# Attention in pairs of units with a written order on every engine, half of expert 0 by seven products, and Sinkhorn steps between matmuls

## The chip, the cores and the metric

The kernel runs on one core of a Trainium2 chip. Its engines are TensorE (PE, with its weight loads shown apart as PEld), VectorE (DVE), ScalarE (ACT), GpSimd (POOL) and SyncE (SP, which only issues transfers here). The metric is device microseconds of one execution. Rows of a profile or trace call a line of the kernel L and its number.

## The reference

Attention, then a mixture of experts whose weights are normalised over rows and columns (Sinkhorn), then a second mixture with two experts for each token. All in float32.

```python
# attention: batch 2, heads 8, sequence 576, head dim 64
scores = scale * np.matmul(q, k.transpose(0, 1, 3, 2))
mask_local = (rel >= 0) & (rel < stride)                      # heads 0-3, stride 32
mask_strided = (rel >= 0) & (pos[None, :] % stride == pos[:, None] % stride)   # heads 4-7
...
attn = attn / (np.sum(attn, axis=-1, keepdims=True) + 1e-09)
x = attention output as (1152, 512)
# first mixture: 8 experts, w1 512x1024, w2 1024x512
P = np.exp(logits)
for _ in range(8):
    P /= P.sum(1, keepdims=True) + 1e-09
    P /= P.sum(0, keepdims=True) + 1e-09
    P *= N / E
for e in range(E):
    h = np.maximum(x @ w1[e], 0.0)
    ye = h @ w2[e]
    out += P[:, e:e + 1] * ye
# second mixture: the same sizes, noisy gate, the two best experts of each token
```

## The kernel before, in words

Every float32 product is made of three products of rounded operands: `split` (L101 to L106) writes the rounded part of a tensor on ACT (`hi`: xh, u1h, gh, ...) and the rest on DVE (`lo`: xl, u1l, gl, ...), and `mm3` (L164) multiplies hi by hi, lo by hi and hi by lo.

**Attention.** The (batch, two heads) blocks are cut into 24 units, 12 of local heads (3 blocks of 96 keys, 288 columns of scores) and 12 of strided heads (4 or 3 blocks of 54 keys, 216 or 162 columns). A unit (`unit`, L210 to L247) runs in this order: scores on PE (`sc`), the negated maximum and its scale on DVE (L231, L232), exponentials with row sums on ACT (L235), two small operations for the reciprocal on DVE (L236, L237), the multiplication by it on POOL (L238), transposes on PE (`tr`, L241), their copy to SBUF on DVE (`at`, L213), the product with the values on PE (`ot`, L247), and the split of the result into xh and xl. Ahead of the scores of the first units stand products of a constant that nobody reads (`hum`, L210): 10 and then 2 for each of the units 1 to 12, 32 in all.

**First mixture.** Expert 0 needs no Sinkhorn weight yet (its weight is multiplied in later, when expert 1 starts). Each expert's 1024 hidden columns are worked in 4 quarters of 256. A quarter of expert 0 is direct: `pair1` makes h (72 products of 384 columns, or as many in other widths), `pair2` makes y (54 products of 512 columns) and adds it to `acc` on DVE. Its tokens 0 to 511 are worked while the second batch's attention runs, the others after it. The quarters of experts 1 to 6 go by a scheme with seven products in place of eight (`Unit`, L665: 84 products of 288 columns for a quarter, and the same 54 of `pair2`). It needs four sums of quarters of x (`sums`: 16 additions on DVE, L622 and L624, then splits into sh and sl) and differences of weights made on POOL (`conv_wino`, L154). Expert 7 and the second mixture follow in another form, which the change leaves alone.

**Gate and Sinkhorn.** `gate_logits` (L320, L324) and `sinkhorn` (L329 to L353) run at a raised priority among expert 0's late tokens. One of the 8 rounds is nine small DVE operations around one product on PE, the column sum `cs` (L348). The small constants (`cs<-in_cst`, another `cs`) are loaded in two transfers; the second one, and `wg_sb`, are issued on ACT's queue at L298 after the ninth unit's split.

**Order.** A scheduler that simulates the program decides the order of each engine's instructions; priorities (`high_priority`) and `issue_after` marks steer it. Each engine runs its own instructions in that order.

## Time and profile before

| what | value |
|---|---|
| three runs | 1116.22, 1117.54, 1119.85 us; median 1117.54 us |
| the profiled execution: its span | 1120.2 us (no other time of it is listed) |
| PE busy | 1102.6 us (98%) |
| DVE, ACT, POOL busy | 665.0, 394.3, 173.8 us |
| attention, gate, Sinkhorn and expert 0 | about the first 175 us |

The span runs from the first to the last instruction of the profiled execution. Busy shares are means over all stages; PE's 98% includes stretches in which it was granted half its clock, and matmuls whose modelled ends overlap. The three runs spread over 0.3%.

### The profile page before, as it was taken

What the parts mean: (1) busy time and instruction counts of PE and PEld (TensorE: products, weight loads), DVE (VectorE), ACT (ScalarE), POOL (GpSimd) and SP (SyncE); (2) the same over time, 40 slices, a digit from 0 to 9 for tenths busy, and PEclk for the clock granted to TensorE, in tenths of its full rate; (3) what the DMA queues carried; (4) which work ended last, traced back from release to release, by engine and by line L of the source; (5) the groups of instructions that cost most, each with busy time, mean ns of one, the idle gap of its engine ahead of it and who ended that gap; (6) DMA issues with size and microseconds to landing.
All of it is one profiled execution on the core that took longest, in us unless ns stands there. A gap on an engine that the chain in (4) does not pass through costs nothing.

```text
span 1120.2 us, 17350 instructions
## 1 busy us (share of the span) xinstructions
PE 1102.6 (98%) x6878; PEld 957.3 (85%) x6878; DVE 665.0 (59%) x1374; ACT 394.3 (35%) x884; POOL 173.8 (16%) x204
## 2 busy tenths in 40 slices
PE   9899999999999999999999999999999999999996
PEld 5677989899998999899999989998888888888885
DVE  5785697666666666666666767553366364544440
ACT  5542144333332333323333323231123263544441
POOL 2110022111112111121111110000041431322211
PEclk9899999999999999999999999999999999999999
DMA  9512135112111121111111111022113682555541
GB/s 278 151 57 75 38 103 159 38 38 75 39 38 38 39 76 38 38 39 38 45 69 38 38 39 56 20 75 75 47 49 88 174 303 41 197 196 194 170 102 23
DMA packets 31216, 96.27 MB, mean 86 GB/s; under 512 B 6522, under 2 KB 15226, under 8 KB 22556
## 3 DMA queue, kind: packets, MB, share of 16 engines
q1 hardware_dynamic: 16028, 78.13, 20.6%
q0 software_dynamic: 5200, 10.17, 4.3%
q10 hardware_dynamic: 9904, 6.83, 2.0%
q8 instruction: 55, 0.90, 0.3%
q14 instruction: 29, 0.24, 0.1%
HBM read 83.60 MB, written 11.60 MB: 85 GB/s over the span
## 4 chain that ended last, share of the span: by engine, by line
PE 87%; DVE 4%; issue 3%; DMA 3%; POOL 2%; ACT 1%; POOLq 0%; ACTq 0%; SPq 0%
PE y L164 40%; PE h L164 16%; PE a L665 14%; PE b L665 7%; PE d L665 3%; PE y L838 2%; PE xgt L750 1%; DMA table<-en,si 1%; PE sc L225 1%; POOL table L498 1%; PE sc L210 1%; PE tr L241 1%; DMA wg_sb<-in_wg 1%; PE ot L247 1%; DMA xg<-x2d,tt 1%
## 5 line engine op out<-in xcount | busy, mean ns | idle before, releaser
L591 DVE SCALAR_TENSOR_TENSOR acc<-y,P,acc 128x512 f32<-128x512 f32 x207 | 152.6, 748 | 141.7 <-PE y L164 141.7
L164 PE MATMUL y<-u2h,gh 128*128 128x512 f32 x504 | 198.3, 394 | 0.3 <-DVE acc L591 0.3
L164 PE MATMUL y<-u2l,gh 128*128 128x512 f32 x504 | 197.1, 391 | 0.0
L164 PE MATMUL y<-u2h,gl 128*128 128x512 f32 x504 | 189.9, 392 | 0.7 <-DVE gl L102 0.6
L154 POOL TENSOR_TENSOR ut<-raw 128x256 f32<-128x256 f32 x48 | 35.6, 762 | 513.2 <-DVE u1l L106 442.0
L164 PEld LDWEIGHTS y<-u2h,gl 128*128 128x128 f32 x504 | 94.3, 188 | 20.9 <-DVE gl L102 2.0
L164 PE MATMUL h<-xl,wh 128*128 128x384 f32 (+8 forms) x352 | 110.2, 313 | 0.0
L164 PE MATMUL h<-xh,wh 128*128 128x384 f32 (+8 forms) x352 | 109.6, 315 | 0.3 <-DVE hl L102 0.3
L164 PE MATMUL h<-xh,wl 128*128 128x384 f32 (+8 forms) x352 | 109.8, 312 | 0.0
L164 PEld LDWEIGHTS y<-u2h,gh 128*128 128x128 f32 x504 | 94.7, 188 | 15.4 <-issue 0.7
L164 PEld LDWEIGHTS y<-u2l,gh 128*128 128x128 f32 x504 | 94.6, 188 | 13.9
L101 ACT ACTIVATE hh<-h 128x256 fp32r<-128x256 f32 (+2 forms) x88 | 35.5, 415 | 97.8 <-PE h L164 97.7
L164 PEld LDWEIGHTS h<-xh,wh 128*128 128x128 f32 x352 | 66.2, 189 | 2.1 <-DVE hl L102 0.6
L164 PEld LDWEIGHTS h<-xl,wh 128*128 128x128 f32 x352 | 66.4, 189 | 1.1 <-issue 0.6
L104 ACT ACTIVATE u2h<-raw 128x1024 fp32r<-128x1024 f32 x31 | 32.8, 1059 | 96.2 <-PE y L164 96.2
L164 PEld LDWEIGHTS h<-xh,wl 128*128 128x128 f32 x352 | 66.3, 188 | 0.0
L102 DVE SCALAR_TENSOR_TENSOR hl<-h,hh 128x256 fp32r<-128x256 f32 (+2 forms) x88 | 40.4, 464 | 38.9 <-ACT hh L101 38.9
L106 DVE TENSOR_TENSOR wl<-raw,wh 128x1024 fp32r<-128x1024 f32 x42 | 49.6, 1221 | 18.7 <-ACT wh L104 18.7
L665 PE MATMUL b<-sh,u1h 128*128 128x288 f32 x192 | 56.9, 296 | 0.0
L665 PE MATMUL a<-sh,u1l 128*128 128x288 f32 x192 | 56.9, 296 | 0.0
L665 PE MATMUL b<-sl,u1h 128*128 128x288 f32 x192 | 56.8, 296 | 0.0
L665 PE MATMUL a<-sl,u1h 128*128 128x288 f32 x192 | 56.7, 295 | 0.0
(248 smaller groups left out, 2502.5 us busy)
## 6 DMA issues: line engine op xcount, KB each, us to landing
raw<-in_u SPq DMA_DIRECT2D x31, 1024.0 KB, 5.0
raw<-in_v SPq DMA_DIRECT2D x20, 1024.0 KB, 10.3
acc<-in_v SPq DMA_DIRECT2D x12, 1024.0 KB, 7.5
raw<-in_w SPq DMA_DIRECT2D x4, 1024.0 KB, 5.3
out<-zero ACTq DMA_DIRECT2D x1, 3072.0 KB, 18.7
x2d<-acc ACTq DMA_DIRECT2D x9, 256.0 KB, 2.0
vs<-in_vL SPq DMA_DIRECT2D x4, 432.0 KB, 11.4
ks<-in_kS SPq DMA_DIRECT2D x4, 297.0 KB, 7.7
```

The lines of the kernel that those rows point to most:

```text
L101: seen[0] = nc.scalar.activation(hi, src, AF.Relu)
L102: nc.vector.scalar_tensor_tensor(lo, src, 0.0, hi.bitcast(F32), op0=ALU.max, op1=ALU.subtract)
L104: seen[0] = nc.scalar.activation(hi, src, AF.Copy)
L106: nc.vector.tensor_tensor(lo, src, hi.bitcast(F32), op=ALU.subtract)
L154: nc.gpsimd.tensor_tensor(t[:, o], x, y, op=ALU.subtract)
L164: nc.tensor.matmul(o, a, b, start=start, stop=stop)
L210: nc.tensor.matmul(o, onesb, onesb[:, None, :].to_broadcast([128, 4, 128]), start=True, stop=True)
L225: nc.tensor.matmul(sc[h * 64:h * 64 + w, i * nk:(i + 1) * nk], qs[r, j * w:(j + 1) * w], ks[r, j * step:j * step + nk], start=False, stop= ...
L241: nc.tensor.transpose(tr[:nk, i * nq:(i + 1) * nq], s[:, i], ident[:nq, :nq])
L591: nc.vector.scalar_tensor_tensor(acc[:, t], p, P[:, t, scale:scale + 1], acc[:, t], op0=ALU.mult, op1=ALU.add)
L665: nc.tensor.matmul(p, l[:, b, c], m, start=first and i == 0, stop=i == 5, skip_group_check=not first)
L838: nc.tensor.matmul(p[j * w:j * w + k, :d], hr[:, f, :k], raws[f // 4][:, f % 4, j * d:(j + 1) * d], start=f == 0, stop=f == 7)
```

## The change

- Attention runs in 12 pairs of units with methods (`Pair`, `Piece`) whose order is written out. In step p, PE makes masks and scores of the new pair, the value products of the old pair and the transposes of the current one; DVE does the maxima of the new pair, the copies of the current one, then reciprocals and splits by turns. The order of all five engines is as written (`manual_schedule`) from the first load to the end of Sinkhorn. The products of the constant are 10 and then 2 for four pairs, 18 in all.
- No product of expert 0 runs before attention's last pair. Quarters 0 and 1 run directly over all tokens in widths of 384; quarters 2 and 3 go by the seven-product scheme, so 26 quarters do where 24 did.
- The first result of `pair2` is copied by ACT instead of DVE. The 16 additions for the sums of x move from DVE to POOL (`add_up`, 8 in each of two calls).
- Sinkhorn becomes a generator, advanced after chosen pieces of expert 0's work; a round has one DVE operation fewer.
- The constants' second transfer and `wg_sb` are issued at the start of step 3; the zeros for the outputs, `wgn`, `noise` and the table are issued after the written stretch, on ACT's queue.

```diff
-        hum(sc, 10 if where[0] == 1 else 2 if where[0] <= 12 else 0)
-        evac(at[:nk, :nb * 2 * w].rearrange("p (b q) -> p b q", q=w), tr[:nk, :nb * nq].rearrange("p (b q) -> p b q", q=64)[:, :, :w])
...
-        for _ in range(8):
+        for k in range(9):
+            if k:
+                p = ps("b", "cs")
+                nc.tensor.matmul(p[:, :E], onesr, c1, start=True, stop=True)
+                c2 = spool.tile([128, E], F32, name="c2")
+                nc.vector.tensor_scalar(c2, p[:, :E], 1e-9, float(E) / N, op0=ALU.add, op1=ALU.mult)
+                nc.vector.reciprocal(c2, c2)
+                nc.vector.tensor_tensor(P, P, c2[:, None, :].to_broadcast([128, NT, E]), op=ALU.mult)
+            if k == 8:
+                return
...
         elif first:
-            nc.vector.tensor_copy(acc[:, t], p)
+            nc.scalar.activation(acc[:, t], p, AF.Copy)
...
-    for q in range(NP):
-        raw = fetch_u(0, q)
-        with tc.issue_after(firsts[min(q, 1) * 3 + 8].ins):
-            a, b = conv_u1(raw[0]), conv_u2(raw[1])
-        pair1(a, early)
-        for t in range(4):
-            pair2(b, t, None, q == 0)
...
+    def add_up(c):
+        r = tpool.tile([128, 4, HALF], F32, tag="r", name="r")
+        for i in range(4):
+            nc.gpsimd.tensor_tensor(r[:, i], quarter[0][i][:, c].bitcast(F32), quarter[1][i][:, c].bitcast(F32), op=ALU.add)
+        for o, x, y, op in ((3, 2, 3, ALU.add), (2, 0, 2, ALU.subtract), (0, 3, 0, ALU.subtract), (1, 1, 0, ALU.subtract)):
+            nc.gpsimd.tensor_tensor(r[:, o], r[:, x], r[:, y], op=op)
+        for k, i in enumerate((3, 0, 2, 1)):
+            sums.append(partial(split, sh[:, k, c], sl[:, k, c], r[:, i]))
...
+        for p in range(-1, n + 1):
+            if p == 3:
+                nc.scalar.dma_start(cs[:, C_U:], cst[:, C_U:])
+                nc.scalar.dma_start(wg_sb, wg)
...
+            for i, u in enumerate(new):
+                u.mask((10 if p < 0 else 2 if p < 4 else 0) if i == 0 else 0)
+            for u in new:
+                u.scores()
+            for u in new:
+                u.top()
+            for u in new[:1]:
+                u.exps()
+            for u in old:
+                u.out()
+            if p == n - 1:
+                pair1(u1, whole[:1])
...
+            for u in cur:
+                u.turn()
+            for u in cur:
+                u.keep()
+            if p == n - 1:
+                gate_products(0, "d")
+            for u in new[:1]:
+                u.norm()
+            for u in old[:1]:
+                u.put()
+            for u in new[1:]:
+                u.exps()
+            for u in new[1:]:
+                u.norm()
+            for u in old[1:]:
+                u.put()
...
+        for k, chunk in enumerate(chunks):
+            chunk()
+            if k < 3 or k % 2 == 0:
+                next(sink, None)
...
+            if k == 9:
+                add_up(1)
+                side[-1:-1] = sums
+            if k in (1, 2, 4, 6, 7, 8, 9, 11, 13, 15, 17, 18, 19, 20, 21):
+                side.pop(0)()
...
-    for e in range(1, E - 1):
-        for q in range(NP):
-            raw = fetch_u(e, q)
-            a, b = conv_wino(raw[0]), conv_u2(raw[1])
+    for e, q in [(e, q) for e in range(E - 1) for q in range(NP)][2:]:
+            if e or q > 2:
+                raw = fetch_u(e, q)
+                u1, u2 = conv_wino(raw[0]), conv_u2(raw[1])
+            a, b = u1, u2
```

The methods of `Piece` hold the same operations as `unit` did: `top` L231 and L232, `exps` L235, `norm` L236 to L238, `turn` L241, `keep` the copy of L213, `out` L247, `put` the split of the result.

Three places of the engines' orders. First POOL, from the attention on. Rows read: the line, the operation, what it writes and reads; `s` is a unit's exponentials, `en`, `meta`, `upper` and `fold` are small tables that come from the constants `cs`. Before:

```order
L302 ISA
L302 TENSOR_TENSOR fold<-cs 64x8
L303 TENSOR_TENSOR fold_97<-cs 128x16
L305 TENSOR_TENSOR fold_97<-fold_97,cs 128x16 x2
L238 TENSOR_TENSOR s<-s,sm 128x288 x6
L238 TENSOR_TENSOR s<-s,sm 128x216 x2
L238 TENSOR_TENSOR s<-s,sm 128x162
L238 TENSOR_TENSOR s<-s,sm 128x216 x2
L238 TENSOR_TENSOR s<-s,sm 128x162
L300 CAST upper<-cs 128x128
L394 CAST en<-cs 128x6 x3
L510 COPY meta<-cs 128x3
```

POOL after, the same place and on to the first weight differences:

```order
L269 TENSOR_TENSOR s<-s,sm 128x288 x6
L269 TENSOR_TENSOR s<-s,sm 128x216 x2
L641 MEMSET wg_95 128x256
L393 CAST en<-cs 128x6 x3
L509 COPY meta<-cs 128x3
...
L698 TENSOR_TENSOR fold_96<-fold_96,cs 128x16 x2
L609 TENSOR_TENSOR r<-xh,xl 128x576 x4
L611 TENSOR_TENSOR r<-r 128x576 x4
L153 TENSOR_TENSOR ut<-raw 128x256 x2
L153 TENSOR_TENSOR ut<-raw,ut 128x256 x2
L609 TENSOR_TENSOR r<-xh,xl 128x576 x4
L611 TENSOR_TENSOR r<-r 128x576 x4
```

The casts that read the late constants stood behind the twelfth unit's multiplication and now stand behind the eighth's; the additions of `add_up` now stand here, on either side of the first weight differences.

Second DVE, one round of Sinkhorn in the middle of expert 0 (`c` is the column sum or its reciprocal, `rs` the row sum, `gl` the rest of h). Before:

```order
L350 TENSOR_SCALAR c_1481<-cs 128x8
L351 RECIPROCAL c_1481<-c_1481 128x8
L352 TENSOR_SCALAR c_1481<-c_1481 128x8
L353 TENSOR_TENSOR P<-P,c_1481 128x72
L341 TENSOR_REDUCE rs<-P 128x9
L102 SCALAR_TENSOR_TENSOR gl<-h,gh 128x320
L342 TENSOR_SCALAR rs<-rs 128x9
L343 RECIPROCAL rs<-rs 128x9
L344 TENSOR_TENSOR P<-P,rs 128x72
L346 TENSOR_REDUCE c_1491<-P 128x8
```

After:

```order
L340 TENSOR_SCALAR c_1476<-cs 128x8
L341 RECIPROCAL c_1476<-c_1476 128x8
L342 TENSOR_TENSOR P<-P,c_1476 128x72
L346 TENSOR_REDUCE rs<-P 128x9
L347 TENSOR_SCALAR rs<-rs 128x9
L348 RECIPROCAL rs<-rs 128x9
L349 TENSOR_TENSOR P<-P,rs 128x72
L105 TENSOR_TENSOR u1l<-raw,u1h 128x512
L351 TENSOR_REDUCE c_1485<-P 128x8
L105 TENSOR_TENSOR u1l<-raw,u1h 128x256
L102 SCALAR_TENSOR_TENSOR gl<-h,gh 128x384
```

The scale by N / E has gone, and splits of weights stand between the round's operations.

Third PE, where one column sum stands among the products of `pair1` (h), 336 places after PE's first instruction in the program. After:

```order
L171 MATMUL h<-xl,u1h 128x384
L171 MATMUL h<-xh,u1l 128x384
L338 MATMUL cs<-c_1440,onesr 128x8
L171 MATMUL h<-xh,u1h 128x384
L171 MATMUL h<-xl,u1h 128x384
```

The product reads DVE's `c` of that round, and PE's next products of h stand behind it. Before, each such product stood where the scheduler had put it; after, it stands behind a chosen piece of expert 0.

## Rows read from the trace of the kernel before

**Rows 1.** The page: busy time of the engines, bytes moved, one group of POOL.

```profile
PE 1102.6 (98%) x6878; PEld 957.3 (85%) x6878; DVE 665.0 (59%) x1374; ACT 394.3 (35%) x884; POOL 173.8 (16%) x204
...
GB/s 278 151 57 75 38 103 159 38 38 75 39 38 38 39 76 38 38 39 38 45 69 38 38 39 56 20 75 75 47 49 88 174 303 41 197 196 194 170 102 23
...
L154 POOL TENSOR_TENSOR ut<-raw 128x256 f32<-128x256 f32 x48 | 35.6, 762 | 513.2 <-DVE u1l L106 442.0
```

**Rows 2.** The chain that ended last: start us, us, what, how many.

```profile
1.13 5.81 PE sc L210 x16
...
79.95 1.39 PE lgT L320 x8
...
307.43 5.45 PE y L164 x24
...
401.47 5.45 PE y L164 x24
...
738.09 2.11 PE h L164 x12
...
741.59 14.56 PE h L164 x84
```

**Rows 3.** Groups of PE over the span, shapes apart: busy us, mean ns.

```profile
L324 PE MATMUL lgt<-fold,lt 64*128 64x8 f32 x18 | 2.5, 256 | 0.0
...
L348 PE MATMUL cs<-c,onesr 128*128 128x8 f32 x16 | 2.3, 214 | 0.0
```

**Rows 4.** Groups of DVE, 0 to 185 us, shapes apart.

```profile
L595 DVE TENSOR_TENSOR acc<-y,acc 128x512 f32<-128x512 f32 x27 | 17.9, 684 | 5.2 <-PE y L164 5.1
...
L106 DVE TENSOR_TENSOR u1l<-raw,u1h 128x512 fp32r<-128x512 f32 x16 | 10.5, 672 | 3.5 <-ACT u1h L104 3.5
...
L106 DVE TENSOR_TENSOR sl<-r,sh 128x576 fp32r<-128x576 f32 x8 | 6.9, 889 | 0.0
...
L213 DVE COPY at<-tr 96x384 f32<-96x384 f32 x12 | 6.6, 547 | 2.2 <-PE tr L241 2.1
...
L231 DVE TENSOR_REDUCE nmx<-sc 128x3 f32<-128x288 f32 x12 | 5.4, 449 | 9.0 <-PE sc L225 9.0
...
L213 DVE COPY at<-tr 54x432 f32<-54x432 f32 x8 | 4.8, 598 | 3.0 <-PE tr L241 3.0
...
L106 DVE TENSOR_TENSOR xl<-ot,xh 128x216 fp32r<-128x216 f32 x8 | 4.4, 553 | 0.9 <-ACT xh L104 0.8
...
L106 DVE TENSOR_TENSOR xl<-ot,xh 128x192 fp32r<-128x192 f32 x12 | 4.2, 348 | 0.6 <-ACT xh L104 0.6
...
L236 DVE TENSOR_SCALAR sm<-sm 128x3 f32<-128x3 f32 x16 | 3.4, 210 | 2.7 <-ACT s L235 2.7
...
L231 DVE TENSOR_REDUCE nmx<-sc 128x4 f32<-128x216 f32 x8 | 2.9, 368 | 0.0
```

**Rows 5.** Timeline of DVE, the first reduction of scores.

```profile
8.12 0.46 DVE L231 TENSOR_REDUCE nmx<-sc 128x3 f32<-128x288 f32 x1 [8.12 <-PE sc L225]
```

**Rows 6.** Timeline 30 to 44 us, rows of ACT's queue, POOL and PE.

```profile
30.18 0.34 ACTq L298 DMA_DIRECT2D cs<-in_cst  x1
...
39.56 0.29 POOL L300 CAST upper<-cs 128x128 bf16<-128x128 f32 x1 [8.85 <-DMA cs<-in_cst]
...
41.04 0.53 PE L241 MATMUL tr<-cs,s 128*96 128x128 f32 x3 [2.84 <-POOL s L238]
...
43.28 0.87 PE L241 MATMUL tr<-cs,s 128*96 128x128 f32 x3 [0.61 <-POOL s L238]
```

**Rows 7.** Windows of 2 us: engines busy, granted clock, DMA share, GB/s.

```profile
40.00:42.00 2.00, 0.96 (x12) 0.74 (x14) 1.11 (x4) 1.87 (x10) 0.98 (x4) 1.00 0.37 156
...
44.00:46.00 2.00, 2.00 (x22) 1.46 (x22) 1.97 (x6) 1.99 (x8) 0.30 (x1) 0.50 0.00 0
```

**Rows 8.** Timeline at 160.8 us, POOL and DVE side by side.

```profile
160.81 1.95 POOL L154 TENSOR_TENSOR ut<-raw 128x256 f32<-128x256 f32 x2 [16.81 <-DVE u1l L106]
...
161.06 2.31 DVE L106 TENSOR_TENSOR sl<-r,sh 128x576 fp32r<-128x576 f32 x2
```

More of the change, by code (lines that the diff above doesn't have):

```diff
@@ L300, in tile_kernel @@
-    nc.gpsimd.tensor_copy(upper, cs[:, C_U:C_U + 128])
-    nc.gpsimd.memset(wg2.bitcast(F32), 0.0)
-    nc.gpsimd.tensor_tensor(fold, ident[:64, :E], ident[:64, 32:32 + E], op=ALU.add)
-    nc.gpsimd.tensor_tensor(fold2, ident[:, :2 * E], ident[:, 32:32 + 2 * E], op=ALU.add)
-    for j in (64, 96):
-        nc.gpsimd.tensor_tensor(fold2, fold2, ident[:, j:j + 2 * E], op=ALU.add)
-    where[1] = "a"
-    attention(1)
-    split(wg2[:, :, :E], wg2[:, :, 32:32 + E], wg_sb)
-    lt = [apool.tile([64, 384], F32, tag=f"lt{g}", name=f"lt{g}", bufs=1) for g in range(3)]
@@ L569, in tile_kernel, with pair1 @@
     late = ((512, 320), (832, 320))
-    def pair1(w, groups):
+    def pair1(w, groups, js=range(2)):
         wh, wl = w
-        for j in range(2):
+        for j in js:
             for o, n in groups:
@@ L617, in sums @@
-    def sums():
-        with tc.tile_pool(name="tpool", bufs=1, side="right", reuse_waits="tile") as tpool:
-            for c in range(2):
-                r = tpool.tile([128, 4, HALF], F32, tag="r", name="r")
-                for i in range(4):
-                    nc.vector.tensor_tensor(r[:, i], quarter[0][i][:, c].bitcast(F32), quarter[1][i][:, c].bitcast(F32), op=ALU.add)
-                for o, x, y, op in ((3, 2, 3, ALU.add), (2, 0, 2, ALU.subtract), (0, 3, 0, ALU.subtract), (1, 1, 0, ALU.subtract)):
-                    nc.vector.tensor_tensor(r[:, o], r[:, x], r[:, y], op=op)
-                for k, i in enumerate((3, 0, 2, 1)):
-                    split(sh[:, k, c], sl[:, k, c], r[:, i])
@@ L628, in tile_kernel @@
[L628 to L646 removed]
+    raw0 = []
```

374 lines of the change are left out of this document (214 added, 160 removed).

## The prediction

> **What bounds the kernel now.** I read the engines' busy times first, then the chain that ended last, then the groups of the first 185 us, then the timeline where the chain leaves PE. PE is busy for 98% of the span [rows 1], and the chain shows why: it goes from one group of products to the next, and in the experts the same piece comes back every (401.47 - 307.43) = 94.04 us for four quarters, so 23.51 us for a quarter by seven products [rows 2]. Expert 7's first products begin at 741.59 - 2.11 = 739.48 us [rows 2], with 24 such quarters behind them: 24 x 23.51 = 564.2. What lies ahead (attention, gate, Sinkhorn, expert 0) therefore takes 739.48 - 564.2 = 175.2 us. Everything after expert 6 is the same program in both kernels, so the change is worth what these 175.2 us and two more quarters become.
>
> PE was full there too, but not always at speed. The constants' second transfer is issued at 30.18 and lets POOL's cast go at 39.56, 9.4 us later; a unit's multiplication stands behind that cast on POOL, so PE stands idle for 2.84 us ahead of its transposes [rows 6]. At 40 to 42 us the granted clock is 1.00, at 44 to 46 us 0.50, which is the lower of the two levels, 1.2 GHz [rows 7]; three transposes go from 0.53 to 0.87 us [rows 6].
>
> **Expert 0's quarters.** A direct quarter is 72 products of 384 columns at 14.56 / 84 = 0.173 us, 12.5 us, and 54 of 512 columns at 5.45 / 24 = 0.227 us, 12.3 us [rows 2]: 24.8 us. By seven products it costs 23.5. Two quarters change, so PE has 2 x 1.3 = 2.6 us less to do. Widths of 384 in place of 512 and 320 carry the same columns and are costed at nothing.
>
> **Attention by itself.** With no expert work between units, PE has too little to do in a pair, and DVE sets the pace. A local unit costs DVE 0.449 (maximum) + 3 x 0.21 (three small ones) + 0.547 (copy) + 0.348 (split) = 1.97 us, a strided one 0.368 + 0.63 + 0.598 + 0.553 = 2.15 [rows 4]; a pair 3.95 and 4.30. I add 0.25 for each pair, for hand-overs between engines, a choice between nothing and the 0.9 at which this would eat the whole gain with the waits below. The first maximum comes at 8.12 [rows 5] behind 16 products of the constant that take 5.81 [rows 2]; with 10 it would come 2.2 us sooner, less about 0.6 for the second unit's scores: 6.5. From there to the last pair's step are 11 steps, 6 x 4.20 + 5 x 4.55 = 48.0. Splits of weights that DVE does on the way are about 4 of 512 columns, 4 x 0.672 = 2.7 [rows 4], of which I count 2.3. Attention ends for PE, which from then on has products in hand, at 6.5 + 48.0 + 2.3 = 56.8 us. The 14 products of the constant that go lie in PE's idle time and bring nothing more than the first six.
>
> **What PE then still has.** Two direct quarters without a gap: h 2 x 12.5 = 25.0, y 2 x 12.3 = 24.6. The gates' products 3 x 1.39 = 4.2 [rows 2], their folds 2.5 and the column sums 2.3 [rows 3]; the last pair's transposes and value products about 2.2 (7 x 0.18 [rows 6] and 1.0). Together 60.8. So expert 0's direct part ends at 117.6; two quarters by seven products add 47.0: 164.6 against 175.2. **With no wait at all the change is worth 10.6 us.** The copies that move from DVE to ACT, one DVE operation fewer in each round and the hoisted transfers cost nothing: ACT is busy for 35% [rows 1], and the queues move under 80 GB/s for long stretches after 28 us [rows 1].
>
> **What waits.** First, the constants. They are issued in step 3, at 6.5 + 3 x 4.2 = 19 to 20 us, and POOL's casts now stand behind the eighth unit's multiplication. Ahead of that transfer the code asks for four pairs, a weight quarter and a fifth pair, about 6.2 MB; at 278 GB/s [rows 1] some 5.5 MB have come by then, so the constants land 2 us of backlog and some 2 of their own later, at 24; if they take 9.4 as before [rows 6], at 29. The ninth unit's multiplication is wanted at about 23. Behind it on POOL all later ones queue, and PE's transposes, DVE's copies and splits with them. Bounds 0 and 6 us; I take 2, near the backlog's own figure.
>
> Second, Sinkhorn. The direct part after the folds, about 41 us, holds on DVE 8 rounds x 8 small operations x 0.21 = 13.4, nine additions to acc x 0.684 = 6.2, ten rests of h at 384 / 512 x 0.684 = 0.51, 5.1, splits of 4864 columns of weights at 0.672 / 512 = 6.4, and eight of 576 columns for the sums, 8 x 0.756 = 6.1 [rows 4]: 37.2 of 41. Each column sum stands in PE's order and the next h or y stand behind it; a round's last DVE operation that is late by a split keeps PE by that split. Meanwhile POOL makes the second eight additions, each 576 / 256 x 0.762 = 1.71 us by the page's group [rows 1], 13.7 in all. Beside POOL two of DVE's splits took 2.31 together, 1.16 each, where 0.756 would be the rate alone [rows 8, 4]: half as much again. If 40% of DVE's work in those 13.7 us has both inputs in SBUF, that is 2.8 us more, so 40 of 41. Bounds: 0, if the chunks leave room, and 13.7, if DVE loses every addition's time; I take 4, nearest to what rows 8 give.
>
> The Trainium skill (SBUF — State Buffer, "Who interferes with whom") speaks against moving these additions: a VectorE instruction with two SBUF inputs and a GpSimd instruction that reads SBUF hold a shared port pair by turns, for a whole instruction each. The trace agrees in kind [rows 8]; by that rule taken to its end the stretch would lose about 13.7 us instead of my 4.
>
> **Sum.** 10.6 - 2 - 4 = 4.6 us less than the profiled 1120.2, 1115.6. That execution lies 2.7 us above the median of the three runs, so I forecast 1112.9 as a median. About 0.3% is what a measurement here can tell from no change: 1114.2 to 1120.9.
>
> **The rivals.**
> - *POOL waits for the constants, and the clock falls (slower).* If they land after about 27 us, PE stands idle for 3 us or more, as in the 2.84 us that came before the lower clock [rows 6, 7]. Nothing dense follows in the written order until attention's last pair, so the clock may stay at 0.50; a pair's PE work, 8 transposes at 0.18 [rows 6] and an estimated 2.0 of scores and value products, 3.4 us, becomes some 5.6 (0.87 / 0.53 [rows 6]) and passes DVE's 4.5: 1.1 more for each of 6 pairs, 6.6. Then 10.6 - 5.5 - 6.6 - 4 = -5.5: 1125.7 in the profile, 1123.0 as a median. For it: just this happened once. Against it: less traffic lies ahead of the transfer than its 9.4 us would need.
> - *DVE becomes the bound in the Sinkhorn stretch (slower).* Decides when DVE's work there passes 44 us, that is, when POOL's additions cost it over 7 us. At 12 us of waits: 10.6 - 2 - 12 = -3.4, a median of 1120.9. For it: 37 of 41 us are full without any slowing. Against it: the first eight additions run beside operations that read PSUM, and rows 8 show a half more, not a full stop.
> - *No gain that can be measured.* The hand-overs cost 0.8 for each pair instead of 0.25: 6 us more, and the gain of 4.6 becomes a loss of 1.4, a median of 1118.9. For it: each step hands a unit through PE, DVE, ACT and POOL and back, in one written order. Against it: two pairs are in flight.
> - *Everything hides.* The waits come to 0 to 2: a gain of about 9.5, a median of 1108.
>
> **Chances.** The forecast's own case (a gain of 2 to 8, medians 1109.5 to 1115.5) 0.50; everything hides 0.15; no gain 0.13; DVE bound 0.12; constants and clock 0.10. Faster than 1114.2: 0.43 of the first and all of the second, 0.58. Within the band: 0.07 of the first, 0.10 of "no gain" and 0.04 of "DVE bound", 0.21. Slower: 0.21. For 8 in 10 the range runs from 1105.5, a little below "everything hides" (a pair at DVE's bare times brings another 2.7 us), to 1123, the slower rival's figure; the forecast's own range is 1109.5 to 1115.5.
>
> **What would show it.** In the profile after: the last pair's step, the first product of pair1 on PE, at 55 to 59 us; the seven-product rhythm still 23.5 with 26 quarters, and expert 7 at 728 to 736 us; POOL's first cast of en ending idle time by the DMA of cs, under 3 us; PE's idle time ahead of the column sums 2 to 6 us in all, released by DVE; the granted clock at 1.00 but for a few us. The forecast is wrong if a pair takes over 5 us, if PEclk falls for more than 10 us inside attention, if the gaps at the column sums exceed 10 us, or if a quarter of expert 0 by seven products takes longer than 23.5 because its sums come late.

## The result and the profile after

The change made the kernel slower: 1132.61 us, the median of 4 runs (1131.80 to 1133.54), against 1118.69 for the kernel before (4 runs, 1116.22 to 1125.70). The ratio is 1.0104 with a 95% interval of 1.0074 to 1.0134. The profiled execution took 1133.54, with a span of 1131.7. The forecast was 1112.9 with a range up to 1123, so the time lies outside it, on the other side of the kernel before, and beyond the slowest rival (1123.0).

The page of the profile after, the lines that answer to [rows 1], with the granted clock (PEclk) by slices of 28 us:

```profile
PE 1099.0 (97%) x6888; PEld 965.7 (85%) x6888; DVE 658.5 (58%) x1350; ACT 396.4 (35%) x898; POOL 198.7 (18%) x228
...
PEclk9889999999999999999999999999999899999998
...
GB/s 245 129 177 38 50 63 39 38 38 54 59 38 38 38 43 71 39 38 38 75 38 38 38 39 52 23 85 65 56 52 74 173 279 62 195 193 192 164 106 23
```

PE is busy for 3.6 us less, and the span is 11.5 longer: PE's idle time rose from 1120.2 - 1102.6 = 17.6 us to 1131.7 - 1099.0 = 32.7, and a product at the lower clock counts as busy all the while. The share of 97% hides both. The chain that ended last, the pieces that answer to [rows 2]:

```profile
360.09 5.46 PE y L171 x24
...
454.13 5.46 PE y L171 x24
...
743.72 2.11 PE h L171 x12
...
747.22 14.56 PE h L171 x84
```

The rhythm of the experts is what it was, (454.13 - 360.09) / 4 = 23.51 us for a quarter. By the prediction's reckoning expert 7 starts at 747.22 - 2.11 = 745.11 (its first 12 products run earlier, among the last y products of expert 6, and are taken off), so what lies ahead of the 24 quarters of experts 1 to 6 takes 745.11 - 564.2 = 180.9 us: it was 175.3 in the profile before, and 164.6 in the sum without a wait. What comes after expert 7's start takes 1131.7 - 745.1 = 386.6, against 1120.2 - 739.5 = 380.7, with the same instructions.

The first part can be cut in three. On the timeline of PE, the first product of `pair1`, with which attention no longer sets PE's pace, and the last y product of the two direct quarters:

```profile
60.02 0.69 PE L171 MATMUL h<-xh,u1h 128*128 128x384 f32 x1
...
133.78 0.39 PE L171 MATMUL y<-u2h,gl 128*128 128x512 f32 x1
```

Attention takes 60.0 us (forecast without a wait: 56.8), the direct quarters 73.8 (60.8), the two quarters by seven products the remaining 180.9 - 133.8 = 47.1 (47.0). So the surplus of 16.3 us shows up as 3.2 in attention and 13.0 in the direct quarters. The last term agrees in part by luck: 18 seven-product products of the two later quarters, at 0.13 us each 2.4 us, already stand in the direct part, and PE idles for 1.0 us behind it.

**Attention.** The first reduction of scores, [rows 5], came at 6.80 (forecast 6.5), so the shorter start works. Then the constants. The timeline of ACT's queue, POOL and PE, for [rows 6]:

```profile
6.80 0.46 DVE L256 TENSOR_REDUCE nmx<-sc 128x3 f32<-128x288 f32 x1 [6.80 <-PE sc L247]
...
19.92 0.34 ACTq L638 DMA_DIRECT2D cs<-in_cst  x1
...
28.02 0.44 POOL L393 CAST en<-cs 128x6 int32<-128x6 f32 x3 [5.83 <-DMA cs<-in_cst]
...
29.05 1.69 PE L276 MATMUL tr<-cs,s 128*54 128x128 f32 x7 [2.40 <-POOL s L269]
```

The constants landed about 8 us after their issue, at 28.0 where the forecast had 24. PE stood idle for 2.40 us ahead of its transposes, and the granted clock was then 0.50, the lower level. Windows of 2 us, columns as in [rows 7]:

```profile
24.00:26.00 2.00, 0.87 (x26) 0.67 (x20) 1.19 (x7) 1.32 (x9) 0.00 (x0) 1.00 1.04 255
...
28.00:30.00 2.00, 0.95 (x5) 0.72 (x6) 0.07 (x1) 1.29 (x8) 1.48 (x6) 0.50 1.02 233
30.00:32.00 2.00, 2.00 (x16) 1.39 (x16) 1.60 (x5) 0.00 (x0) 0.16 (x1) 0.50 0.97 244
...
86.00:88.00 2.00, 2.00 (x8) 1.80 (x7) 0.00 (x0) 0.50 (x1) 0.00 (x0) 0.50 0.00 0
...
116.00:118.00 2.00, 0.40 (x3) 0.40 (x4) 2.00 (x4) 1.95 (x4) 1.92 (x2) 1.00 0.00 0
...
120.00:122.00 2.00, 2.00 (x6) 1.54 (x6) 1.76 (x9) 0.29 (x1) 0.00 (x0) 0.50 0.00 0
```

The last three lines are from the direct quarters: there the clock falls too, once after the gate's folds and once after a wait at a column sum. Added up over all windows of 2 us, attention has about 13 us at the lower level; more than 10 was one of the prediction's own signs of being wrong. It costs little by itself, as e3 will show.

**The direct quarters.** Groups of PE and DVE, shapes apart, for [rows 3, 4]; the small DVE operations are one round of Sinkhorn, eight times:

```profile
L338 PE MATMUL cs<-c,onesr 128*128 128x8 f32 x16 | 2.6, 234 | 3.7 <-DVE c L351 3.7
...
L349 DVE TENSOR_TENSOR P<-P,rs 128x72 f32<-128x72 f32 x8 | 4.2, 521 | 0.3
L347 DVE TENSOR_SCALAR rs<-rs 128x9 f32<-128x9 f32 x8 | 3.4, 423 | 0.3
L342 DVE TENSOR_TENSOR P<-P,c 128x72 f32<-128x72 f32 x8 | 2.9, 368 | 0.3
L351 DVE TENSOR_REDUCE c<-P 128x8 f32<-128x72 f32 x8 | 2.3, 289 | 0.2
```

PE now waits 3.7 us for DVE ahead of the column sums; before it did not wait there at all [rows 3]. The timeline shows why the round is late. First PE, then DVE, then POOL:

```profile
110.91 0.39 PE L338 MATMUL cs<-c,onesr 128*128 128x8 f32 x2 [0.82 <-DVE c L351]
...
117.60 0.39 PE L338 MATMUL cs<-c,onesr 128*128 128x8 f32 x2 [1.69 <-DVE c L351]
```

```profile
103.35 0.17 DVE L347 TENSOR_SCALAR rs<-rs 128x9 f32<-128x9 f32 x1
...
103.81 0.23 DVE L349 TENSOR_TENSOR P<-P,rs 128x72 f32<-128x72 f32 x1
...
108.08 1.03 DVE L347 TENSOR_SCALAR rs<-rs 128x9 f32<-128x9 f32 x1
...
109.39 1.15 DVE L349 TENSOR_TENSOR P<-P,rs 128x72 f32<-128x72 f32 x1
110.57 0.28 DVE L351 TENSOR_REDUCE c<-P 128x8 f32<-128x72 f32 x1
...
114.04 1.16 DVE L347 TENSOR_SCALAR rs<-rs 128x9 f32<-128x9 f32 x1
```

```profile
106.26 5.55 POOL L609 TENSOR_TENSOR r<-xh,xl 128x576 f32<-128x576 f32 x4 [26.44 <-DVE sl L105]
111.89 6.74 POOL L611 TENSOR_TENSOR r<-r 128x576 f32<-128x576 f32 x4
```

At 103 us, without POOL, the scale of rs takes 0.17 and the multiplication 0.23. Beside POOL's additions of 1.4 to 1.7 us each they take 1.03 to 1.16, and the two of a round make it 1.8 us longer. The reductions keep their 0.28.

### The profile page after: what moved, and what is told of

It reads as the page before. It is cut to its first block, busy times and chain, and to the rows that moved or that the text cites. A ratio compares the mean times of both kernels' runs of the same rounds, so it can differ in the third digit from the quotient of the medians.

```text
span 1131.7 us, 17401 instructions
## 1 busy us (share of the span) xinstructions
PE 1099.0 (97%) x6888; PEld 965.7 (85%) x6888; DVE 658.5 (58%) x1350; ACT 396.4 (35%) x898; POOL 198.7 (18%) x228
## 4 chain that ended last, share of the span: by engine, by line
PE 86%; DVE 4%; issue 3%; DMA 3%; ACT 2%; POOL 2%; POOLq 0%; SPq 0%; ACTq 0%; DVEq 0%
PE y L171 40%; PE a L763 15%; PE h L171 14%; PE b L763 7%; PE d L763 4%; PE y L937 2%; PE xgt L849 1%; DMA table<-en,si 1%; ACT s L262 1%; POOL table L497 1%; DMA acc<-in_qL 1%; DMA xg<-x2d,tt 1%; PE ot L289 1%; PE tr L276 1%; DVE u1l L105 0%
## 5 line engine op out<-in xcount | busy, mean ns | idle before, releaser
L171 PE MATMUL y<-u2h,gl 128*128 128x512 f32 x504 | 192.7, 392 | 0.0
L171 PEld LDWEIGHTS y<-u2l,gh 128*128 128x128 f32 x504 | 94.9, 188 | 13.7
L763 PE MATMUL a<-sh,u1h 128*128 128x288 f32 x208 | 61.6, 296 | 1.0 <-ACT s L769 1.0
L104 ACT ACTIVATE u2h<-raw 128x1024 fp32r<-128x1024 f32 x28 | 29.7, 1061 | 91.7 <-PE y L171 91.7
L763 PE MATMUL a<-sh,u1l 128*128 128x288 f32 x208 | 61.6, 296 | 0.0
L763 PE MATMUL b<-sh,u1h 128*128 128x288 f32 x208 | 61.5, 296 | 0.0
L763 PE MATMUL b<-sl,u1h 128*128 128x288 f32 x208 | 61.5, 296 | 0.0
L763 PE MATMUL a<-xh,u1l 128*128 128x288 f32 x208 | 61.5, 295 | 0.0
```

The lines of the kernel that those rows point to most:

```text
L104: seen[0] = nc.scalar.activation(hi, src, AF.Copy)
L171: nc.tensor.matmul(o, a, b, start=start, stop=stop)
L763: nc.tensor.matmul(p, l[:, b, c], m, start=first and i == 0, stop=i == 5, skip_group_check=not first)
```

## The experiments

In the table, "attention" is the time of the first `pair1` product, "direct" the time from there to the end of the direct quarters, "two quarters" the time on to the end of expert 0's last y product (2.6 us more than in the reckoning above, since expert 1's first products start ahead of it), "first part" the start of expert 7 less 564.2, "behind attention" the first part less attention, and "rest" the span less that start. All are from the profiled execution; the ratio is from all runs, against the kernel before on the same chip.

| kernel | ratio, 95% | attention | direct | two quarters | first part | behind attention | rest |
|---|---|---|---|---|---|---|---|
| before, the profile of [rows 1] |  |  |  |  | 175.3 |  | 380.7 |
| before, profiled again (e8) | 1.0008, 0.9979 to 1.0036 |  |  |  | 168.7 |  | 386.3 |
| after | 1.0104, 1.0074 to 1.0134 | 60.0 | 73.8 | 49.7 | 180.9 | 120.9 | 386.6 |
| after, profiled again (e14) | 1.0134, 1.0103 to 1.0165 | 60.9 | 73.7 | 49.7 | 181.7 | 120.8 | 384.8 |
| e1, constants first | 1.0085, 1.0058 to 1.0111 | 56.6 | 74.2 | 49.7 | 177.9 | 121.3 | 384.7 |
| e2, half the sums left out | 1.0085, 1.0068 to 1.0102 | 61.2 | 69.1 | 49.7 | 177.4 | 116.2 | 385.8 |
| e3, constant's products in all pairs | 1.0104, 1.0087 to 1.0121 | 59.4 | 73.5 | 49.7 | 180.0 | 120.6 | 384.4 |
| e4, Sinkhorn later | 1.0103, 1.0086 to 1.0119 | 61.2 | 64.8 | 58.4 | 180.8 | 119.6 | 385.9 |
| e5, before with constants first | 1.0041, 1.0023 to 1.0059 |  |  |  | 176.0 |  | 380.1 |
| e6, four edits together | 1.0087, 1.0054 to 1.0119 | 58.2 | 75.5 | 48.3 | 179.4 | 121.2 | 388.3 |
| e7, two quarters direct again | 1.0107, 1.0076 to 1.0138 | 60.4 | 73.6 * | 52.4 * | 178.5 | 118.1 | 384.5 |
| e9, three idle loads | 1.0114, 1.0066 to 1.0162 | 61.1 | 74.0 | 49.7 | 182.2 | 121.1 | 382.6 |
| e10, Sinkhorn spread | 1.0063, 1.0041 to 1.0086 | 57.0 | 66.6 | 57.2 | 176.2 | 119.2 | 388.5 |
| e11, late fills | 1.0105, 1.0065 to 1.0145 | 59.1 | 73.7 | 48.2 | 180.0 | 120.9 | 384.3 |
| e12, before with sums on POOL | 1.0006, 0.9988 to 1.0023 |  |  |  | 168.0 |  | 382.4 |
| e13, planned after attention | 1.0111, 1.0081 to 1.0140 | 59.8 | 66.5 | 61.0 | 183.8 | 124.0 | 381.5 |

The border between "direct" and "two quarters" is blurred, because some products of the next quarters run ahead of it: 18 of 288 columns in most kernels, 13 in e4 and e10, 12 in e13. In e7 (*) it is so blurred that the two columns don't compare. "Behind attention" is free of this; the kernels whose edits lie elsewhere (after, e14, e3, e9, e11) have 120.6 to 121.1 there. The attention column of the kernels with attention unchanged (after, e2, e4, e7, e9, e11, e14) runs from 59.1 to 61.2.

**e1: are the constants the attention's surplus?** The second transfer moves to the start of the kernel.

```diff
         nc.scalar.dma_start(cs[:, :C_U], cst[:, :C_U])
+        nc.scalar.dma_start(cs[:, C_U:], cst[:, C_U:])
+        nc.scalar.dma_start(wg_sb, wg)
...
             if p == 3:
-                nc.scalar.dma_start(cs[:, C_U:], cst[:, C_U:])
-                nc.scalar.dma_start(wg_sb, wg)
-            if p == 3:
```

> The second transfer of the constants and wg_sb are issued right behind the first one, at the start, instead of in step 3. Theory (POOL's casts wait 5.83 us for the constants at 22 to 28 us, PE stands idle behind them and loses its clock at 26 to 33 us): POOL's wait goes, PE's idle time at 24 to 31 us and the low clock behind it go, attention ends about 5 us sooner and the whole is 5 to 8 us shorter, 1125 to 1128. Rival (DVE and the loads set the pace of attention anyway, the wait was cover for something else): under 2 us.

Attention ended at 56.6, which is the forecast's figure without this stall, and the first part became 3.0 us shorter, not the 5 to 8 expected. The same edit stands in e10, e6 and e13, where attention ended at 57.0, 58.2 and 59.8. So the constants explain most of attention's surplus, and DVE's pace was estimated well; that it fits to 0.2 us is chance. Between the ratios of e1 and after the intervals don't decide.

**e2: what do POOL's late additions cost?** The second `add_up` fills r with zeros and leaves its eight additions out, so half the sums of x are missing from the output.

```diff
+        if c:
+            nc.gpsimd.memset(r, 0.0)
-        for i in range(4):
+        for i in range(0 if c else 4):
...
-        for o, x, y, op in ((3, 2, 3, ALU.add), (2, 0, 2, ALU.subtract), (0, 3, 0, ALU.subtract), (1, 1, 0, ALU.subtract)):
+        for o, x, y, op in () if c else ((3, 2, 3, ALU.add), (2, 0, 2, ALU.subtract), (0, 3, 0, ALU.subtract), (1, 1, 0, ALU.subtract)):
```

> Leaves out the second eight additions on POOL (the sums of half the columns are zeros, written by one memset). Theory (POOL's additions hold VectorE's small operations up for a whole addition each, so the column sums come late and PE waits 4.8 us and loses clock): the small operations between 106 and 127 us take 0.17 to 0.23 us each, the three waits ahead of column sums shrink below 1 us in all, 5 to 7 us gained, 1126 to 1128. Rival (VectorE's stretch is full by its own work): 0 to 2 us gained, the waits stay.

The direct part fell from 73.8 to 69.1, and the time behind attention from 120.9 to 116.2: the additions cost 4.7 us. PE's waits ahead of the column sums shrank from 3.7 to 1.4 us. The same two groups of DVE as above, now beside no addition for most of their time:

```profile
L349 DVE TENSOR_TENSOR P<-P,rs 128x72 f32<-128x72 f32 x8 | 2.2, 277 | 0.3
L347 DVE TENSOR_SCALAR rs<-rs 128x9 f32<-128x9 f32 x8 | 1.9, 237 | 0.3
```

**e3: the clock in attention.** Three products of the constant stand in every pair, as filling for PE.

```diff
-                u.mask((10 if p < 0 else 2 if p < 4 else 0) if i == 0 else 0)
+                u.mask((10 if p < 0 else 3) if i == 0 else 0)
```

> Three products of the constant ahead of every pair's scores (18 become 43). Theory (in attention it is the fall of the granted clock behind idle time that costs, at 46 to 51 and 56 to 65 us): the granted clock stays at 1.00 there, attention's last part and the first products of h run at full rate, 3 to 6 us gained, 1127 to 1130. Rival (the idle times are waits for VectorE that three products of 0.23 us don't fill, the clock falls all the same): no gain, or 1 to 2 us lost.

The mean granted clock of attention rose from 0.89 to 0.97, but the first part became only 0.9 us shorter, no more than attention varies between profiles, and the ratio did not move. That fits a PE which waits for DVE anyway: a product at the lower clock then mostly fills time that would have been a wait.

**e4: the column sums moved off the direct quarters.** Sinkhorn's steps stand behind three pieces of each half quarter by seven products.

```diff
             chunk()
-            if k < 3 or k % 2 == 0:
-                next(sink, None)
...
-        assert next(sink, 0) == 0 and not side
+        assert not side
...
                 x.p1()
+                next(sink, None)
...
                 x.p6()
+                next(sink, None)
...
                 x.p7()
+                next(sink, None)
```

> The steps of Sinkhorn stand in the two seven-product quarters of expert 0, outside the written stretch, in place of between the chunks of the direct quarters. Theory (PE waits in its order for column sums that VectorE makes late): PE's waits at 109, 115 and 125 us go, and VectorE has room in the seven-product stretch (half busy there); 5 to 8 us gained, 1125 to 1128. Rival (the waits only move to the new place, or the sums' splits come late there): under 2 us gained.

The direct part fell by 9.0 us, to 64.8, and the two quarters grew by 8.7, to 58.4. Five products fewer ahead of the border are 0.7 of the 9.0, so the price of Sinkhorn in the direct part is about 8.3 us, of which the forecast had 2.3 for the products and 4 for waits. Most of it follows Sinkhorn to its new place: behind attention only 1.3 us are gained.

**e5: would the kernel before gain from early constants?** The transfer no longer waits for the ninth split.

```diff
-    with tc.issue_after(firsts[8].ins):
-        nc.scalar.dma_start(cs[:, C_U:], cst[:, C_U:])
-        nc.scalar.dma_start(wg_sb, wg)
+    nc.scalar.dma_start(cs[:, C_U:], cst[:, C_U:])
+    nc.scalar.dma_start(wg_sb, wg)
```

> The kernel before, with the second transfer of the constants and wg_sb issued right behind the first at the start. Theory (POOL's wait for the constants costs the kernel before 2.84 us of idle PE and 5 us of clock): no idle time at 38 us, granted clock 1.00 up to 60 us, 5 to 8 us gained, 1110 to 1113. Rival (the scheduler's order only shifts the wait): under 2 us. It is also a second look at the gathers after expert 7 with the old first part: if the 5.9 us that the changed kernel lost there belong to its first part, the time behind expert 7's start stays at 381 us here; if they come and go with a transfer's latency, it may be 384 to 386 here as well.

It is 0.4% slower. The wait at the transposes of [rows 6] is down from 2.84 to 0.23 us, but others took its place; the timeline of PE:

```profile
10.74 0.71 PE L225 MATMUL sc<-ks,acc 64*64 64x96 f32 x12 [2.03 <-DMA acc<-in_qL]
...
40.05 0.53 PE L241 MATMUL tr<-cs,s 128*96 128x128 f32 x3 [0.23 <-POOL s L238]
...
76.66 0.50 PE L164 MATMUL y<-u2h,gl 128*128 128x512 f32 x1 [1.04 <-DVE gl L102]
```

**e6: four edits together**: the constants first, three products of the constant in every pair, the split of `u2` one pair later, and Sinkhorn's steps closer together with the second `add_up` behind them.

```diff
...
-            if p == 10:
+            if p == 11:
                 u2 = conv_u2(raw0[0][1])
...
-            if k < 3 or k % 2 == 0:
+            if k < 3 or k in (4, 6, 8, 9, 10, 11, 12, 13):
...
-            if k == 9:
+            if k == 11:
                 add_up(1)
```

> The changed kernel with four edits: constants first, three products of the constant for every pair, the splits of quarter 0's second weights behind the last pair in place of the eleventh, Sinkhorn's steps closer together with the second eight additions behind most of them. Theory (waits in the written order and the clock behind them are the whole loss of the first part): idle time and lost clock from 0 to 145 us fall from 29 us to about 17, the first part ends 8 to 10 us sooner, 1122 to 1125. Rival (another wait follows each one that is taken away): 1127 to 1130, as with one edit.

A miss: the first part is 1.5 shorter than after, half of what the constants alone gave. With the steps closer together PE's waits ahead of the column sums rose to 5.2 us, and the direct part to 75.5.

**e7: the seven-product quarters by themselves.** The last two quarters of expert 0 are direct again.

```diff
-                u1, u2 = conv_wino(raw[0], side), conv_u2(raw[1], side)
+                u1, u2 = conv_u1(raw[0], side), conv_u2(raw[1], side)
...
-            if k in (1, 2, 4, 6, 7, 8, 9, 11, 13, 15, 17, 18, 19, 20, 21):
+            if k in (1, 2, 4, 6, 7, 8, 9, 11, 13, 15, 17, 18, 19, 20):
...
+    for q in (2, 3):
+        if q > 2:
+            raw = fetch_u(0, q)
+            u1, u2 = conv_u1(raw[0]), conv_u2(raw[1])
+        pair1(u1, whole)
+        for t in range(NT):
+            pair2(u2, t, None)
+    for e, q in [(e, q) for e in range(1, E - 1) for q in range(NP)]:
...
```

> The changed kernel with quarters 2 and 3 of expert 0 direct, as before the change. Theory (the term of the sum: 1.3 us for a quarter by seven products, PE is dense there): 2 to 3 us slower than the changed kernel, 1134.5 to 1136. Rival (the seven-product quarters wait for sums and the saving is lost): within 1 us of it, or faster.

In the time of the whole kernel nothing can be told (1.0107 against 1.0104). In the profile the two quarters take 52.4 instead of 49.7 us, but not for the same work: 36 products of h of the third quarter stand ahead of the direct part's end, and 66 products of expert 1 ahead of the last y, where after has about 27. From attention's end to expert 7 the kernel with direct quarters is faster, 118.1 against 120.9 and 120.8 (e14). A direct quarter's products of h need no sums of x, and with them PE waits for only 1.2 us ahead of the column sums instead of 3.7, and not at all in the two quarters instead of 1.0. So the saving of 2.6 us that the forecast counted does not show in this kernel: the waits take more than that.

**e8 and e14: both kernels profiled again**, without an edit, since the sum had been made against one execution.

> The kernel before once more, for a second trace of it. Theory (its profiled execution was an unlucky one: the constants came late and the clock fell at 43 to 53 us; after expert 7's start its time is steady): span about 1116, granted clock 1.00 at 44 to 52 us, first part about 171 us by the chain's reckoning, 380 to 381 us behind expert 7's start. Rival (what lies behind expert 7 varies by itself): 383 us or more there.

> The changed kernel once more, beside the kernel above on the same chip. Theory (the time behind expert 7's start goes one of two ways by chance): its first part 180 to 182 us as before, behind expert 7's start 380 to 383 or 384 to 388 us, runs spread over 1127 to 1134. Rival (the long way belongs to the changed kernel): all runs at 1131 to 1134.

The kernel before has a first part of 168.7 us this time, not 175.3, and nothing falls: windows of 0 to 60, 60 to 100 and 100 to 145 us, first of this execution and then of the kernel after.

```profile
0.00:60.00 60.00, 57.74 (x690) 39.79 (x692) 43.96 (x141) 36.57 (x170) 16.82 (x40) 1.00 0.69 206
60.00:100.00 40.00, 39.39 (x295) 29.61 (x290) 26.02 (x58) 12.97 (x40) 2.13 (x4) 1.00 0.17 58
100.00:145.00 45.00, 45.00 (x250) 40.12 (x249) 32.79 (x88) 12.51 (x23) 3.71 (x4) 1.00 0.14 48
```

```profile
0.00:60.00 60.00, 47.54 (x727) 36.34 (x727) 40.74 (x142) 34.15 (x185) 16.75 (x41) 0.89 0.67 177
60.00:100.00 40.00, 38.96 (x218) 34.30 (x217) 16.33 (x47) 12.89 (x25) 15.39 (x15) 0.91 0.44 131
100.00:145.00 45.00, 40.19 (x219) 35.85 (x218) 40.48 (x87) 16.69 (x32) 17.80 (x16) 0.96 0.18 66
```

The wait and the lower clock of [rows 6, 7] thus belong to some executions of the kernel before and not to all. The kernel after, profiled again, repeats itself: 181.7 us. In its first 60 us PE idles for 12.5 us, where e8 has 2.3: no product of expert 0 stands between the units any more. The prediction had counted this, as DVE's pace.

**e9 and e11: the rest behind expert 7.** It is the same program in both kernels, yet 380.7 and 386.6 us long. e9 fetches three weight quarters a second time that nothing uses, which moves each later transfer on by three places in the buffers' rotation; e11 holds the late transfers of ACT's queue until 117.7 to 119.9 us. The code of after names them behind the written stretch, but the scheduler moved the tables up to 1.7 to 3.5 us and the zeros of the outputs to 59.4 and 60.0; before issues them at 159.5 to 161.7.

```diff
+            if e in (2, 3, 4) and q == 1:
+                fetch_u(e, q)
```

```diff
-    nc.scalar.dma_start(wgn_sb, wgn)
-    nc.scalar.dma_start(noise_sb, noise)
-    nc.scalar.dma_start(table, dummy)
+    with tc.issue_after(seen[0].ins):
+        nc.scalar.dma_start(wgn_sb, wgn)
+        nc.scalar.dma_start(noise_sb, noise)
+        nc.scalar.dma_start(table, dummy)
...
```

> The changed kernel with three more loads of a weight quarter that nobody reads, during experts 2 to 4, so that the transfers behind expert 7 stand at the same place of the queues' rounds and buffers as before the change (28 loads of quarters of u became 31 again). Theory (the 4 to 7 us lost behind expert 7's start come from the transfers' shifted places): 380 to 381.5 us behind expert 7's start, 1127 to 1129 in all. Rival (they come from something else, the gathers land late as in the seven runs of the changed kernel so far): 384 to 388 us there, 1131 to 1134 in all.

> The changed kernel with wgn, noise, the table's and the outputs' zeros issued as before the change, behind the last split of the written stretch (about 130 us) and not at 2 and at 59 us. Theory (the hoisted transfers are what makes the gathers behind expert 7 late more often): 380 to 382 us behind expert 7's start, 1126 to 1129. Rival (those gathers are early or late by chance, the transfers cost nothing where they are): 384 to 388 us or a mixture, 1130 to 1134, the first part unchanged within 1 us.

Neither changed the time. The rest was 382.6 in e9 and 384.3 in e11. What differs is on PE's timeline: how long PE waits for gathers of the second routing. One of them, in the profile after first, then in the two profiles of the kernel before, [rows 1]'s and e8's:

```profile
897.80 0.41 PE L849 MATMUL xgt<-cs,xg 88*128 88x88 f32 x1 [2.78 <-DMA xg<-x2d,tt]
```

```profile
888.93 0.30 PE L750 MATMUL xgt<-cs,xg 88*128 88x88 f32 x1 [0.98 <-DMA xg<-x2d,tt]
```

```profile
886.41 0.37 PE L750 MATMUL xgt<-cs,xg 88*128 88x88 f32 x1 [2.76 <-DMA xg<-x2d,tt]
```

Over the sixteen profiles the rest grows with PE's waits for these gathers: 380.1 us where they come to 0.6 (e5), 382.4 at 2.5 (e12), 384.8 at 3.5 (e14), 386.6 at 4.2 (after), 386.3 at 4.3 (e8), 388.3 at 5.8 (e6); only e10 has 388.5 at 3.0. The kernel before can have the long rest too, so the change is not needed for it. Of the twelve profiles of after and its variants ten have a rest of 384 us or more, of the four of before and its variants one. Why it came more often is open.

**e10: Sinkhorn spread.** The constants first, three products of the constant in every pair, the later `u2`, and one step of Sinkhorn behind each of several long pieces of the seven-product quarters.

```diff
...
-            if k < 3 or k % 2 == 0:
+            if k in (0, 1, 2):
...
                 x.p1()
+                next(sink, None)
...
                 x.p2()
+                next(sink, None)
...
                     y[k]()
+                    if k in (2, 5):
+                        next(sink, None)
```

> The changed kernel with constants first, three products of the constant for every pair, the splits of quarter 0's second weights behind the last pair, and Sinkhorn's rounds one by one in the two seven-product quarters. Theory (each round costs PE only where its column sum stands behind late VectorE work; with 4 us between rounds none does): direct quarters 64 to 66 us from their first product, the seven-product ones 50 to 52, expert 7 at 735 to 738, and 1122 to 1125 in all with 384 to 386 behind it. Rival (Sinkhorn costs its 9 us wherever it stands): 58 us for the seven-product quarters, 1127 to 1130.

The best of the variants of after, 0.6% slower than before. The direct part fell by 7.2 us and the two quarters grew by 7.5, 2.7 of them by 20 more seven-product products that fall into them. PE's waits ahead of the column sums all but went, from 3.7 to 0.7 us, but PE waited for other results of DVE instead, 2.9 us of it in the two quarters. Against e1, which has the constants first as well, 2.1 us are gained behind attention.

**e12: POOL's additions in the kernel before.** All sixteen sums move from DVE to POOL there, and nothing else.

```diff
-                    nc.vector.tensor_tensor(r[:, i], quarter[0][i][:, c].bitcast(F32), quarter[1][i][:, c].bitcast(F32), op=ALU.add)
+                    nc.gpsimd.tensor_tensor(r[:, i], quarter[0][i][:, c].bitcast(F32), quarter[1][i][:, c].bitcast(F32), op=ALU.add)
...
-                    nc.vector.tensor_tensor(r[:, o], r[:, x], r[:, y], op=op)
+                    nc.gpsimd.tensor_tensor(r[:, o], r[:, x], r[:, y], op=op)
```

> The kernel before with one part of the change alone: the 16 additions for the sums of x on POOL in place of DVE. Theory (POOL's additions hold DVE's operations up, but only a written order makes PE wait for it; the scheduler's order has room): within 0.3% of the kernel before, with single small operations of DVE at 0.5 to 1.3 us beside the additions. Rival (the contention costs wherever the additions stand): 4 to 7 us slower.

No change (1.0006, so within about 2.6 us), although DVE is held up there as well; its timeline beside the additions, and PE's:

```profile
137.27 1.22 DVE L352 TENSOR_SCALAR c<-c 128x8 f32<-128x8 f32 x1
...
145.30 1.28 DVE L344 TENSOR_TENSOR P<-P,rs 128x72 f32<-128x72 f32 x1
```

```profile
144.17 0.42 PE L164 MATMUL h<-xh,u1h 128*128 128x320 f32 x1 [1.70 <-DVE gl L102]
```

PE does not wait at a column sum there, but it waits for another result of DVE: 3.1 us between 125 and 185 us, against 0.8 in e8. So the additions are not free in the kernel before either; they cost PE less there than the 4.7 us of e2, too little for these runs to tell.

**e13: the planner instead of the written order.** The written order ends with the gate; Sinkhorn, the direct quarters and the sums are scheduled, with Sinkhorn at a raised priority (and the constants first, three products in each pair, the later `u2`).

```diff
...
+    with tc.high_priority(1500):
+        for _ in sinkhorn():
+            pass
+    a, b = conv_u1(raw0[1][0]), conv_u2(raw0[1][1])
+    pair1(u1, whole[2:])
+    for t in range(3, NT):
+        pair2(u2, t, None, True)
...
```

> Constants first, three products of the constant for every pair, the second weights' splits behind the last pair, and the written order ends with the gate: Sinkhorn, the sums and the rest of the direct quarters are ordered by the scheduler as before the change. Theory (what the change loses behind attention, 13 us over dense PE, comes from the written places of Sinkhorn's column sums and of POOL's additions): from the first product of h to the end of the direct quarters 62 to 66 us in place of 73.8, expert 7 at 731 to 735, 1119 to 1124 in all. Rival (PE has nothing to put beside attention any more, so DVE's and POOL's work of this stretch costs it however it is ordered): 69 us or more, 1126 to 1130.

Not faster: 1.0111. The direct part took 66.5 us, but then the scheduler put the last column sums one behind the other, with no product between them. The timeline of PE, and a window there:

```profile
134.25 0.60 PE L338 MATMUL cs<-c,onesr 128*128 128x8 f32 x2 [2.07 <-DVE c L351]
136.91 0.60 PE L338 MATMUL cs<-c,onesr 128*128 128x8 f32 x2 [2.07 <-DVE c L351]
139.57 0.60 PE L338 MATMUL cs<-c,onesr 128*128 128x8 f32 x2 [2.06 <-DVE c L351]
```

```profile
136.00:138.00 2.00, 0.60 (x2) 0.50 (x2) 1.14 (x7) 0.00 (x0) 0.00 (x0) 0.50 0.00 0
```

Behind attention it took 124.0 us, 3.1 more than after. So giving this stretch to the scheduler, at this one priority, does not win the loss back; that no other order would is not shown.

## Why the prediction was wrong

**The step that failed first: the time to beat.** The sum took 175.2 us for the first part of before, from an execution in which PE idled and the clock fell [rows 6, 7]; e8 and e12 show 168.7 and 168.0. With no wait at all the change is worth 168.7 - 164.6 = 4.1 us, not 10.6, and with the forecast's own waits of 6 it loses 1.9 instead of gaining 4.6. Taking the gain from the median of the runs did not mend this: a gain against a slow execution was taken off runs most of which are not slow. (The 2.7 us also set a span against times; a time here lies 1.8 above its span, 1133.54 against 1131.7, so the profiled execution was some 4.5 above the median.) The rows of one execution can't show this. Of 67 later executions of the kernel before whose mean granted clock is on record, four have 0.993 or less, as the profiled one had; where it fell in them is not known.

**"The constants: I take 2."** They cost about 3 (e1; attention's surplus was 3.2). They landed at 28.0, near the upper end of 29, not at 24. The first rival's place and its limit of 27 us were right, and the clock fell to 0.50; but it came back, so of the rival's 5.5 + 6.6 us only the smaller part was paid.

**"Sinkhorn: I take 4."** It cost 8.3 (e4), less 2.3 of products that were counted: 6.0. POOL's additions made 4.7 of the 8.3 (e2), by the mechanism of the second rival, at less than its 12. The estimate was that DVE's two-input work beside POOL takes half as much again; the rows show small operations of 0.17 to 0.23 us lengthened to over 1 us, each by more than half an addition, and those stand exactly in the round that PE waits for. The Trainium skill (SBUF — State Buffer, "Who interferes with whom") states an exclusive lock for a whole instruction, for `tensor_scalar` in its two-port modes as well, while reductions are free of it on trn2. The trace agrees on each in kind: 0.17 to 1.03 and 1.16, 0.23 to 1.15, and 0.28 for the reduction. Taken over the whole stretch that rule gave 13.7 us, which was too much: the additions cost 4.7.

**What stood in no term: the clock in the direct part, and work that moved into it.** e4 without Sinkhorn still takes 64.8 us where the sum, less the products of the column sums, has 58.5. Of these 6.3 us PE idles for 1.0, loses 63.7 x 0.05 = 3.2 to a mean granted clock of 0.95, and 13 products of the next quarter take 1.7; 0.4 are left. In the profile after the clock is 0.93 over the direct part. It starts low behind attention's last wait (0.50 at 58 to 60 us) and falls again behind the folds and behind a wait at a column sum. The sum counted every product at the full clock.

**"Two quarters change, so PE has 2.6 us less to do."** As a time this is not shown: with the two quarters direct again the stretch behind attention was 2.8 us shorter (e7), with fewer waits on PE.

**What was right.** Attention's pace by DVE (56.8; 56.6 in e1, 57.0 in e10), so the rival with costlier hand-overs falls; the rhythm of 23.51; and PE's wait ahead of the column sums (2 to 6; 3.7). Together: 164.6 + 3.2 + 13.0 + 0.1 = 180.9, where 13.0 = 6.0 + 0.7 + 6.3, the 0.7 being the five products by which after has more than e4 ahead of the border. Against e8's 168.7 that is 12.2 of the 13.9 us between the medians; the rest behind expert 7, which the sum took as equal, varies by some 8 us between the profiles and holds the remainder, by subtraction.

**What stays open.** Why Sinkhorn costs the kernel before so little is not shown. Attention does not cover it there: in e8 attention's last product is at 78.3 us and the eight column sums are at 102.9 to 165.6, in after at 69.5 and 94.5 to 127.4. What differs is the room: 62.7 us of products of h and y that need no column sum, against 32.9. In e8 PE idles for 0.6 us between 60 and 100 us and not at all between 100 and 145. But e10 spread the sums over 59.9 us, which gained only 2.1, so room alone does not explain it. In the places tried the two quarters grew by 8.7, 7.5 and 11.3 us (e4, e10, e13), of which 1.6, 2.7 and 1.7 are seven-product products that fall into that stretch instead of another. No version beat the kernel before.

## What to carry to other kernels

Before summing against one profiled execution, ask whether its own idle time and clock falls recur; a gain made of them is not there in the next run. A latency chain (small operation, product, small operation) that stands in a written order is paid for by the engine behind it; moving the chain to another place moved most of its price along here. When small DVE operations sit in such a chain, count up to a whole POOL instruction of waiting for each that POOL overlaps, not a percentage. And when two variants are cut into stretches, count what work lies in each stretch before the stretches are compared.

## What the runs showed of the hardware beyond that

- A DVE operation with one input, 0.17 us without POOL, took 1.16 beside a POOL addition of 1.4 to 1.7, while the reciprocal right behind it, also with one input, kept its 0.22; so the number of inputs alone does not tell which operations are held up.
- PE busy without a gap with eight-column products can be followed by the lower clock. The timeline of PE after, and the windows behind the gate's 18 folds:

```profile
81.77 2.17 PE L317 MATMUL lgt<-fold,lt 64*128 64x8 f32 x18
```

```profile
84.00:86.00 2.00, 2.00 (x9) 2.00 (x10) 0.39 (x2) 0.00 (x0) 0.00 (x0) 0.66 0.00 0
```

  At 86 to 88 us it is 0.50, and products of 384 columns go from 0.34 to 0.52 us. The four profiles of before and its variants run the same folds in three groups of six (76.4, 87.5 and 90.7 us in e8), and the clock stays at 1.00 there. Of the eleven profiles with all 18 together ten show the fall; in e6 the clock stays at 1.00 behind them, so the folds alone do not decide it.
- The same gather, with the same program ahead of it, let PE wait for 0.98 us in one execution and 2.76 in another; the time behind expert 7's start rose with such waits, from 380.1 us at 0.6 us of waiting in all (e5) to 388.3 at 5.8 (e6).
